# V cache loads issued from ScalarE's DMA queue, K cache loads from SyncE's

## Chip, cores, metric

One core of one Trainium2 chip runs the kernel; the other cores are idle. The metric is device time in microseconds (us) of one execution. Before: 1345.22 us (median of 4 runs, 1344.23 to 1347.4).

## The reference, cut

One decode step of grouped-query attention over a long cache, mixed with a small token MLP that takes almost no time here. Only the attention matters for the argument:

```python
# x [1,1,448], k_cache and v_cache [1, 8, 65536, 256] bfloat16, 16 query heads on 8 kv heads
q = (x @ wq)                                   # 16 heads x 256
p = softmax(einsum("bhqd,bhkd->bhqk", q, k) * 256**-0.5)
o = einsum("bhqk,bhkd->bhqd", p, v)
a = o.reshape(1, 1, 4096) @ wo
return g * a + (1 - g) * b                     # b: token MLP, g: a gate
```

K and V are 268 MB each. All of it must be read once, and nothing is reused.

## The kernel before

The cache is cut into 256 chunks of 2048 rows. Loads take two chunks at once (2 MB, 128 pieces of 16 KB, one for each partition). There are two K buffers (KB) and three V buffers (VB) of one load each. In step s, TensorE transposes the K of chunk s, multiplies q with the transposed K of chunk s-1 ("QK"), and multiplies the exponentials of chunk s-2 with V ("PV"):

```python
DC = 2; KB = 2; VB = 3; NB = 4                 # chunks per load; buffers; transpose groups per chunk
...
@block.sync                                    # SyncE issues every load
    ... six small loads, wq ...
    def k_dma(cd):                             # pair cd = chunks 2cd, 2cd+1
        if cd >= KB:
            eng.wait_ge(sem_tr, NB * ((cd - KB) * DC + DC))   # transposes of pair cd-2 done
        eng.dma_start(kbuf[slot cd % KB], ...).then_inc(sem_k[slot], 16)
    def v_dma(cd):
        if cd >= VB:
            eng.wait_ge(sem_pv, (cd - VB) * DC + DC)          # PV of pair cd-3 done
        eng.dma_start(vbuf[slot cd % VB], ...).then_inc(sem_v[slot], 16)
    for cd in range(NCD + 1):                  # K0, K1, V0, K2, V1, K3, V2, ...
        if cd < NCD: k_dma(cd)
        if cd - 1 >= 0: v_dma(cd - 1)
        ... at cd == NCD - 20: wo ...
@block.tensor
    for s in range(NC + 2):
        if s even: wait sem_k                  # K pair landed
        32 transposes of chunk s               # kst <- kbuf
        QK of chunk s-1                        # sps <- ktT
        if s even: wait sem_v                  # V pair landed
        PV of chunk s-2                        # po <- vbuf
@block.scalar                                  # half of the evictions of the transposes, and exp
    for c in range(NC):
        2 evictions of chunk c (ktT <- kst); exp of chunk c-1
```

So K(j+1) and V(j) are issued together, back to back, when the transposes of chunk 2j-1 are done.

The softmax here doesn't subtract the row's maximum and nothing guards it: scores larger than these inputs give would overflow.

Of the kernel before, what the change touches and what calls it, by code (L numbers as in the profile page):

```python
# [11 lines left out]
def bass_gated_mix__gqa_block_cached__mixer_token_mlp__decode_kernel(  # L12
# [29 lines left out]
    P = 128  # L42
    CH = 2048 if T % 2048 == 0 else T
# [3 lines left out]
    NCPH = T // CH  # L47
# [4 lines left out]
    DC = 2  # L52
    assert NC % DC == 0 and NCPH % DC == 0
    NCD = NC // DC
    KB = 2
    VB = 3
# [18 lines left out]
    with ctx:  # L75
        def sb(shape, dt, name):
            return ctx.enter_context(nc.sbuf_tensor(name, shape, dt))
# [4 lines left out]
        def new_sem(name):  # L82
            return ctx.enter_context(nc.semaphore(name))

        kbuf = sb([P, KB, DC, NT, DH], bf16, "kbuf")
        vbuf = sb([P, VB, DC, NT, DH], bf16, "vbuf")
# [52 lines left out]
        sem_v = [new_sem("semv%d" % i) for i in range(VB)]  # L139
# [9 lines left out]
        sem_pv = new_sem("sem_pv")  # L149
# [21 lines left out]
        @block.sync  # L171
        def _(eng):
            eng.dma_start(xrow_b[:, :], x_row_ap).then_inc(sem_misc, 16)
            eng.dma_start(grow_b[:, :], gate_w.rearrange("(a n) -> a n", a=1)).then_inc(sem_misc, 16)
            eng.dma_start(w1row_b[:, :], B_w1[0:1, :]).then_inc(sem_misc, 16)
            eng.dma_start(b1row_b[:, :], B_b1.rearrange("(a n) -> a n", a=1)).then_inc(sem_misc, 16)
            eng.dma_start(w2row_b[:, :], B_w2.rearrange("f a -> a f")).then_inc(sem_misc, 16)
            eng.dma_start(b2_b[:, :], B_b2.rearrange("(a n) -> a n", a=1)).then_inc(sem_misc, 16)
            eng.dma_start(wq_sb, A_wq.rearrange("(kt c) n -> c kt n", c=KCP)).then_inc(sem_wq, 16)

            def k_dma(cd):
                c0 = cd * DC
                g, k = divmod(c0, NCPH)
                slot = cd % KB
                if cd >= KB:
                    eng.wait_ge(sem_tr, NB * ((cd - KB) * DC + DC))
                src = A_k_cache[0, g, k * CH:(k + DC) * CH, :].rearrange("(p n) d -> p (n d)", p=P)
                eng.dma_start(kbuf[:, slot, :, :, :].rearrange("p c n d -> p (c n d)"), src).then_inc(sem_k[slot], 16)  # L188

            def v_dma(cd):  # L190
                c0 = cd * DC
                g, k = divmod(c0, NCPH)
                slot = cd % VB
                if cd >= VB:
                    eng.wait_ge(sem_pv, (cd - VB) * DC + DC)
                src = A_v_cache[0, g, k * CH:(k + DC) * CH, :].rearrange("(p n) d -> p (n d)", p=P)
                eng.dma_start(vbuf[:, slot, :, :, :].rearrange("p c n d -> p (c n d)"), src).then_inc(sem_v[slot], 16)  # L197

            WO_AT = max(0, NCD - 20)
            for cd in range(NCD + 1):  # L200
                if cd < NCD:
                    k_dma(cd)
                if cd - 1 >= 0:
                    v_dma(cd - 1)
                if cd == WO_AT:
                    eng.wait_ge(s_pe_pro, 3)
                    eng.dma_start(wo_sb, A_wo.rearrange("(kt p) n -> p kt n", p=P)).then_inc(sem_wo, 16)

            eng.wait_ge(sem_tail_v, 1)
            eng.dma_start(out_row_ap, out_b[:, :]).then_inc(sem_out, 16)  # L210
            eng.wait_ge(sem_out, 16)
# [261 lines left out]

        @block.scalar
        def _(act):
            act.wait_ge(s_d2a, 1)
            act.sqrt(statb[:, 3:4], statb[:, 2:3])
            act.activation(statb[:, 5:6], statb[:, 4:5], AF.Exp, scale=-1.0).then_inc(s_a2d, 1)

            def b_tanh(kt):  # L480
                slot = kt % NUR
                act.wait_ge(s_u, kt + 1)
                if kt >= NUR:
                    act.wait_ge(s_pb, kt - NUR + 1)
                act.activation(tring[:, slot, :], zring[:, slot, :], AF.Tanh  # L485
                               ).then_inc(s_tanh, 1)

            for c in range(NC):
                slotT = c % KTB
                if c >= KTB:  # L490
                    act.wait_ge(sem_qk, c - KTB + 1)
                for b in range(NB):
                    u2 = NB * c + b
                    if u2 % 2 != 1:
                        continue
                    act.wait_ge(sem_tr, u2 + 1)
                    act.activation(ktT[:, slotT, b, :], kst[:, b, :], AF.Copy).then_inc(sem_eva, 1)  # L497
                ce = c - 1
                if ce >= 0:
                    act.wait_ge(sem_qk, ce + 1)  # L500
                    if ce >= PTB:
                        act.wait_ge(sem_pv, ce - PTB + 1)
                    act.activation(pT[:, ce % PTB, :], sps[:, ce % 2, 0:2 * NT], AF.Exp, scale=scale  # L503
                                   ).then_inc(sem_exp, 1)
                if INTERLEAVE_B:
                    for kt in range(FT):
                        if posT[kt] == c:
                            b_tanh(kt)
            if not INTERLEAVE_B:
                for kt in range(FT):  # L510
                    b_tanh(kt)
            ce = NC - 1
            act.wait_ge(sem_qk, ce + 1)
            if ce >= PTB:
                act.wait_ge(sem_pv, ce - PTB + 1)
            act.activation(pT[:, ce % PTB, :], sps[:, ce % 2, 0:2 * NT], AF.Exp, scale=scale
                           ).then_inc(sem_exp, 1)
# [28 lines left out]
```

## Time and profile before

| what | where in the profile | value |
|---|---|---|
| time, median | timed runs | 1345.2 us |
| DMA share and rate, 60 to 1300 us | windows | 0.99 to 1.00, 407 to 418 GB/s |
| one 16 KB piece, median | the trace's DMA records | 611 ns |
| between landings of 2 MB loads, median | the trace's landings | 4.90 us |
| K and V, issue to landing, median | DMA issues | 10.6 and 15.2 us |

The page of the kernel before: span; busy time; the DMA queue (records, MB, share of 16 engines); the chain of work that ended last, by engine and by line; DMA issues (count, KB each, median us from issue to landing). PE is TensorE's matrix multiplications and PEld its weight loads, DVE is VectorE, ACT ScalarE, POOL GpSimd, SP SyncE; a q behind the name marks the engine's instruction queue, and "issue" is time in which the engine waited for nothing that the profile shows.

```profile
span 1353.2 us, 53303 instructions
...
PE 1190.9 (88%) x25055; PEld 1156.5 (85%) x25055; DVE 405.9 (30%) x690; ACT 549.1 (41%) x786; POOL 1.2 (0%) x10
...
q1 hardware_dynamic: 41454, 544.24, 97.3%
...
DMA 50%; PE 44%; issue 4%; SPq 1%; ACT 0%; DVE 0%; DVEq 0%; ACTq 0%
DMA vbuf<-in_A_v_cache_dram 50%; PE kst L277 28%; PE po L312 9%; PE sps L293 5%; PE den L316 1%; SPq L188 1%; PE sps L339 1%; PE po L322 0%; ACT ktT L497 0%; ACT pT L503 0%; SPq L197 0%; PE den L327 0%; DVE arow_b L467 0%; DVE densum L448 0%; DVE out_b L472 0%
...
kbuf<-in_A_k_cache_dram SPq DMA_DIRECT2D x128, 2048.0 KB, 10.6
vbuf<-in_A_v_cache_dram SPq DMA_DIRECT2D x128, 2048.0 KB, 15.2
wqo<-in_A_wq_dram SPq DMA_DIRECT2D x1, 3584.0 KB, 17.5
...
```

All loads go through one hardware queue (q1), which fills 97.3% of the 16 engines' time. V takes 4.6 us longer than K from issue to landing because it stands behind K in that queue.

Windows of the kernel before. After the stretch and its length come the busy time of each engine, the granted TensorE clock, the DMA share and GB/s:

```profile
...
core 0: us, PE busy (x) PEld busy (x) DVE busy (x) ACT busy (x) POOL busy (x), PEclk, DMA share, GB/s
60.00:200.00 140.00, 128.01 (x2697) 125.18 (x2695) 66.45 (x152) 62.74 (x93) 0.00 (x0) 0.73 1.00 418
200.00:600.00 400.00, 358.98 (x7665) 350.60 (x7664) 109.28 (x158) 166.58 (x237) 0.00 (x0) 0.75 1.00 417
600.00:1000.00 400.00, 361.28 (x7560) 350.64 (x7559) 107.12 (x156) 164.19 (x234) 0.00 (x0) 0.73 0.99 407
1000.00:1300.00 300.00, 261.01 (x5518) 255.38 (x5515) 78.87 (x114) 120.21 (x171) 0.00 (x0) 0.74 1.00 415
...
```

The engines have no time to spare. A load is 8 pieces per engine, and 8 x 611 ns is 4.89 us, just the median gap between landings. TensorE is busy 87 to 91% of the same windows, so it is close behind.

Who waited for whom (total us, times, longest us), and the chain of waits around 620 us (start us, us, what):

```profile
...
PE po L312 <- DMA vbuf<-in_A_v_cache_dram: 57.5, 56, 2.5
...
PE kst L277 <- DMA kbuf<-in_A_k_cache_dram: 12.1, 7, 9.6
...
```

```profile
...
618.27 0.33 SPq L188
618.60 0.04 issue
618.64 14.31 DMA vbuf<-in_A_v_cache_dram
632.95 0.14 issue
633.08 0.99 PE po L312 x32
...
```

TensorE hardly waits for K. It waits for V: the issue of K (0.33 us) and V, 14.31 us until V has landed, then PV.

The first transposes, from the timeline (start us, us, instruction, and in brackets the idle time before it and what ended it):

```profile
...
24.80 1.44 PE L277 MATMUL kst<-ident,kbuf 128*128 128x128 bf16 x12 [1.07 <-DMA kbuf<-in_A_k_cache_dram]
...
```

wq (3.5 MB) goes first, then K0; TensorE's main loop starts at 24.8 us.

### The profile page before, as it was taken

The numbers are of one execution on the slowest core, as the hardware profiler recorded it, in microseconds if no ns is written. First come the engines' busy times: TensorE is split into PE (matmuls) and PEld (weight loads), VectorE is DVE, ScalarE is ACT, GpSimd is POOL, SyncE is SP. The second block draws the span as 40 slices with busy tenths as digits, with TensorE's granted clock in tenths as the row PEclk, the third lists the DMA queues.
The fourth block names the chain that finished last, engine by engine and source line by source line (L and its number), as shares of the span: only waits on it lengthen the run. The fifth ranks groups of instructions, "written<-read, shape, count | busy, mean of one in ns | idle before, by whom it ended". The sixth has DMA issues, their size and how long they took to land.

```text
span 1353.2 us, 53303 instructions
## 1 busy us (share of the span) xinstructions
PE 1190.9 (88%) x25055; PEld 1156.5 (85%) x25055; DVE 405.9 (30%) x690; ACT 549.1 (41%) x786; POOL 1.2 (0%) x10
## 2 busy tenths in 40 slices
PE   4889898989989898989999888998899896888997
PEld 4889898889888898989888888888898896888886
DVE  3783222222222222222222222222222221222222
ACT  2454344434344344444434434433444442443442
POOL 0000000000000000000000000000000000000000
PEclk9677767768677778676787767766867767777777
DMA  9999999999999999999999999999999999999993
GB/s 302 425 423 411 417 419 425 409 422 412 420 416 416 420 405 423 418 420 407 414 399 402 409 404 414 416 382 402 420 422 419 409 423 398 421 417 416 414 417 160
DMA packets 41672, 547.65 MB, mean 405 GB/s; under 512 B 4136, under 2 KB 8235, under 8 KB 8238
## 3 DMA queue, kind: packets, MB, share of 16 engines
q1 hardware_dynamic: 41454, 544.24, 97.3%
q8 instruction: 198, 3.24, 0.9%
q14 instruction: 20, 0.16, 0.0%
HBM read 544.22 MB, written 0.00 MB: 402 GB/s over the span
## 4 chain that ended last, share of the span: by engine, by line
DMA 50%; PE 44%; issue 4%; SPq 1%; ACT 0%; DVE 0%; DVEq 0%; ACTq 0%
DMA vbuf<-in_A_v_cache_dram 50%; PE kst L277 28%; PE po L312 9%; PE sps L293 5%; PE den L316 1%; SPq L188 1%; PE sps L339 1%; PE po L322 0%; ACT ktT L497 0%; ACT pT L503 0%; SPq L197 0%; PE den L327 0%; DVE arow_b L467 0%; DVE densum L448 0%; DVE out_b L472 0%
## 5 line engine op out<-in xcount | busy, mean ns | idle before, releaser
L497 ACT ACTIVATE ktT<-kst 128x1024 bf16<-128x1024 bf16 x512 | 513.5, 1022 | 763.6 <-PE kst L277 763.6
L277 PE MATMUL kst<-ident,kbuf 128*128 128x128 bf16 x8192 | 726.0, 269 | 26.0 <-issue 13.7
L277 PEld LDWEIGHTS kst<-ident,kbuf 128*128 128x128 bf16 x8192 | 667.8, 125 | 38.5 <-issue 17.8
L433 DVE COPY ktT<-kst 128x1024 bf16<-128x1024 bf16 x512 | 352.9, 691 | 906.1 <-PE kst L277 894.8
L312 PE MATMUL po<-pT,vbuf 128*128 128x2 bf16 x8192 | 251.3, 164 | 92.2 <-DMA vbuf<-in_A_v_cache_dram 57.5
L312 PEld LDWEIGHTS po<-pT,vbuf 128*128 128x128 bf16 x8192 | 232.0, 99 | 98.3 <-issue 63.5
L293 PE MATMUL sps<-qT,ktT 128*128 128x2 bf16 x8192 | 255.6, 165 | 21.4 <-issue 21.2
L293 PEld LDWEIGHTS sps<-qT,ktT 128*128 128x128 bf16 x8192 | 250.6, 100 | 21.6 <-issue 21.4
L503 ACT ACTIVATE pT<-sps 128x32 bf16<-128x32 f32 x255 | 50.0, 196 | 16.0 <-PE sps L293 15.6
L316 PE MATMUL den<-pT,ones_col 128*1 128x32 bf16 x256 | 46.4, 181 | 0.0
L316 PEld LDWEIGHTS den<-pT,ones_col 128*1 128x1 bf16 x256 | 20.3, 79 | 7.5 <-issue 3.0
L254 PEld LDWEIGHTS sps<-xcol,wqo 112*128 112x128 bf16 x128 | 3.5, 104 | 8.2 <-issue 8.2
L254 PE MATMUL sps<-xcol,wqo 112*128 112x1 bf16 x128 | 3.6, 165 | 7.8 <-DMA wqo<-in_A_wq_dram 7.8
L339 PE MATMUL sps<-wqo,oTn 128*1 128x448 bf16 x32 | 8.1, 424 | 0.6 <-DVE oTn L460 0.6
L485 ACT ACTIVATE tring<-zring 128x448 bf16<-128x448 bf16 x14 | 8.1, 578 | 0.2 <-DVE zring L413 0.2
L339 PEld LDWEIGHTS sps<-wqo,oTn 128*1 128x1 bf16 x32 | 3.0, 98 | 5.3 <-issue 2.5
L244 PE MATMUL sps<-h_row,ones_row_b 1*128 1x448 bf16 x1 | 0.6, 551 | 6.5 <-DVE h_row L387 6.5
L405 DVE TENSOR_TENSOR wring<-uring 128x448 bf16<-128x448 bf16 x14 | 5.5, 393 | 1.4 <-issue 0.4
L407 DVE TENSOR_TENSOR zring<-wring,uring 128x448 bf16<-128x448 bf16 x14 | 5.5, 393 | 1.0
L422 DVE TENSOR_TENSOR gu<-wring,tring 128x448 bf16<-128x448 bf16 x14 | 5.5, 392 | 1.0
L411 DVE TENSOR_TENSOR zring<-uring,wring 128x448 bf16<-128x448 bf16 x14 | 5.5, 392 | 1.0
L244 PEld LDWEIGHTS sps<-h_row,ones_row_b 1*128 1x128 bf16 x1 | 0.1, 100 | 6.5 <-DVE h_row L387 6.5
(70 smaller groups left out, 51.0 us busy)
## 6 DMA issues: line engine op xcount, KB each, us to landing
kbuf<-in_A_k_cache_dram SPq DMA_DIRECT2D x128, 2048.0 KB, 10.6
vbuf<-in_A_v_cache_dram SPq DMA_DIRECT2D x128, 2048.0 KB, 15.2
wqo<-in_A_wq_dram SPq DMA_DIRECT2D x1, 3584.0 KB, 17.5
wqo<-in_A_wo_dram SPq DMA_DIRECT2D x1, 3584.0 KB, 24.9
xrow_b<-in_A_x_dram SPq DMA_DIRECT2D x1, 0.9 KB
grow_b<-in_gate_w_dram SPq DMA_DIRECT2D x1, 0.9 KB
w1row_b<-in_B_w_dram SPq DMA_DIRECT2D x1, 3.5 KB
b1row_b<-in_B_b_dram SPq DMA_DIRECT2D x1, 3.5 KB
```

The source lines that it names most:

```text
L188: eng.dma_start(kbuf[:, slot, :, :, :].rearrange("p c n d -> p (c n d)"), src).then_inc(sem_k[slot], 16)
L254: ins = pe.matmul(sps[:, 1, j:j + 1], wq_sb[0:KCP, kt, col0:col0 + P], xcol[0:KCP, kt:kt + 1], start=(kt == 0), stop=(kt == KC - 1))
L277: ins = pe.transpose(kst[:, b, j * P:(j + 1) * P], kbuf[:, slot, ck, nt, dh * P:(dh + 1) * P], ident[:, :])
L293: ins = pe.matmul(sps[:, sbk, 2 * nt:2 * nt + 2], ktT[:, slotT, bnk, j * P:(j + 1) * P], qT[:, dh, REP * g:REP * g + REP], start=(dh == 0) ...
L312: pe.matmul(po[:, col:col + REP], vbuf[:, vslot, cv, nt, dh * P:(dh + 1) * P], pT[:, pslot, 2 * nt:2 * nt + 2], start=first, stop=last)
L316: ins = pe.matmul(den[0:1, g * 2 * NT:(g + 1) * 2 * NT], ones_col[:, 0:1], pT[:, pslot, 0:2 * NT], start=(k == 0), stop=(k == NCPH - 1))
L339: ins = pe.matmul(sps[0:1, 1, 0:DM], oTn[:, col:col + 1], wo_sb[:, kt, :], start=(i == 1), stop=(i == nmm))
L405: vec.tensor_tensor(W, U, U, op=ALU.mult)
L433: vec.tensor_copy(ktT[:, slotT, b, :], kst[:, b, :]).then_inc(sem_evd, 1)
L485: act.activation(tring[:, slot, :], zring[:, slot, :], AF.Tanh).then_inc(s_tanh, 1)
L497: act.activation(ktT[:, slotT, b, :], kst[:, b, :], AF.Copy).then_inc(sem_eva, 1)
L503: act.activation(pT[:, ce % PTB, :], sps[:, ce % 2, 0:2 * NT], AF.Exp, scale=scale).then_inc(sem_exp, 1)
```

## The change

The intent: two rings (a ring is here the work that one issuing engine has queued for the 16 DMA engines; the profile lists each as a hardware queue, q1 or q10) feed the 16 engines at once. V moves to ScalarE's queue. To fit ScalarE's program, V(j) is issued after ScalarE's evictions of chunk 2j-2, one step earlier than before; the first three V loads are issued at the very start.

```diff
@@ SyncE @@
-            def v_dma(cd): ...                # as above
-            for cd in range(NCD + 1):
-                if cd < NCD:
-                    k_dma(cd)
-                if cd - 1 >= 0:
-                    v_dma(cd - 1)
+            for cd in range(NCD):
+                k_dma(cd)
                 if cd == WO_AT: ...
@@ ScalarE @@
+            def v_dma(cd): ...                # the same, with act.wait_ge and act.dma_start
+            for cd in range(min(VB, NCD)):
+                v_dma(cd)
             act.wait_ge(s_d2a, 1)
...
                     act.activation(ktT[:, slotT, b, :], kst[:, b, :], AF.Copy).then_inc(sem_eva, 1)
+                if c % DC == 0 and VB <= c // DC + 1 < NCD:
+                    v_dma(c // DC + 1)
```

More of the change, by code (lines that the diff above doesn't have):

```diff
@@ L188, in k_dma @@
                 eng.dma_start(kbuf[:, slot, :, :, :].rearrange("p c n d -> p (c n d)"), src).then_inc(sem_k[slot], 16)
-            def v_dma(cd):
-                c0 = cd * DC
-                g, k = divmod(c0, NCPH)
-                slot = cd % VB
-                if cd >= VB:
-                    eng.wait_ge(sem_pv, (cd - VB) * DC + DC)
-                src = A_v_cache[0, g, k * CH:(k + DC) * CH, :].rearrange("(p n) d -> p (n d)", p=P)
-                eng.dma_start(vbuf[:, slot, :, :, :].rearrange("p c n d -> p (c n d)"), src).then_inc(sem_v[slot], 16)
-            WO_AT = max(0, NCD - 20)
-            for cd in range(NCD + 1):
-                if cd < NCD:
-                    k_dma(cd)
-                if cd - 1 >= 0:
-                    v_dma(cd - 1)
+            WO_AT = max(0, NCD - 20)
+            for cd in range(NCD):
+                k_dma(cd)
                 if cd == WO_AT:
@@ L475, in _, with v_dma @@
         def _(act):
+            def v_dma(cd):
+                c0 = cd * DC
+                g, k = divmod(c0, NCPH)
+                slot = cd % VB
+                if cd >= VB:
+                    act.wait_ge(sem_pv, (cd - VB) * DC + DC)
+                src = A_v_cache[0, g, k * CH:(k + DC) * CH, :].rearrange("(p n) d -> p (n d)", p=P)
+                act.dma_start(vbuf[:, slot, :, :, :].rearrange("p c n d -> p (c n d)"), src).then_inc(sem_v[slot], 16)
+            for cd in range(min(VB, NCD)):
+                v_dma(cd)
             act.wait_ge(s_d2a, 1)
```

## The prediction

> **What bounds the kernel now.** The loads. Windows over 60 to 1300 us give a DMA share of 0.99 to 1.00 at 407 to 418 GB/s. In the packed trace the 16 KB packets of the cache loads take 611 ns (median), so 8 per engine make a 2 MB load 4.89 us; the median gap between successive landings of cache loads is 4.90 us, the mean 5.14. So the rings run without bubbles; lost are slow packets (about 41 us per engine in all), the two 3.5 MB weight loads, and the ends. TensorE is busy 1191 us (88%) at a mean granted clock of 0.74, near 9.2 us of the 10.3 us that a K/V pair takes; it pauses about 1 us per pair at the P·V matmul (L312, timeline), and the chain of waits alternates V load (50%) and TensorE (44%). SyncE is no limit: 0.33 us (K) and 0.43 us (V) per issue, and it waited 1190 us at L188.
>
> **What the change does.** 128 V issues move from SyncE to ScalarE: 125 in the loop, about 0.43 us each, 54 us on an engine busy 549 us, ahead of an exp with over 2 us of slack. Nearly nothing of it is critical. Bytes and buffers stay. [...]
>
> What moves:
> 1. V(j) is issued about one step (5 us) earlier relative to TensorE, after the transposes of chunk 2j-2 instead of 2j-1. With two rings taking turns, K and V each get about half the rate while both are outstanding: a load then takes about 2 x 4.9 = 9.8 us. V landing falls from 15.2 to 10-12 us, K stays near 10 (10.6 now). TensorE's wait moves from V (57 us listed, more under exp and issue) to K (12 us now).
> 2. Start: three V loads (6 MB) compete with wq and K0. K0 landed at 24.7 us; I estimate 31 to 37. V buffers are then full and loads idle a few us: about +4, less about 2 for the earlier first load.
> 3. End: before, the last load was V, landing at 1335.3, TensorE's loop ending 4.3 us later. Now K(127) lands about when V(127) does, and two chunks of transposes follow: about +5.
> 4. Slow packets cluster 1 to 3 us after an issue. Two rings may fill such holes (up to -35 us if all went) or conflict more. I take -6.
>
> Sum: 1346 + 2 + 5 - 6 = about 1347 us. 80% range 1320 to 1370. Chances: faster by over 2% 0.12, within 2% 0.77, slower by over 2% 0.11.
>
> **What would show it.** Right: DMA share still 0.99-1.00 and 405-425 GB/s in the steady windows; two busy hardware queues of equal bytes; 16 KB packets recorded at about 1.2 us; TensorE's waits for V under 20 us and for K at L277 above 60; first transposes after 30 us; V landing 10-12 us. Wrong: windows where the DMA share falls under 0.95 in mid-kernel, or a steady rate above 425 or under 395 GB/s.
>
> **What would make it wrong.** Two read streams at once disturbing HBM or the engines (slower); the second ring hiding the slow packets (faster); unfair turns that starve K until V's buffers are full and the engines idle; ScalarE held at an issue.

The turns of two rings (item 1) and the 1.2 us for a piece were assumptions. The trace of the change, taken later, shows what there is of them: while both rings held 16 KB pieces not yet started (853 of the 1000 us from 100 to 1100 us), K's ring started 12.8 and V's 11.9 per us; the median piece took 611 ns.

## The result

The change took 1401.58 us (median of 4, 1389.84 to 1405.52) against 1345.22 us. The ratio is 1.0406 (95% interval 1.0361 to 1.0452): slower by 4%. The result lies outside the predicted range of 1320 to 1370 us.

The page after (lines of the program have moved by 12: L277 is L265, L312 is L300):

```profile
span 1397.9 us, 53303 instructions
...
PE 1150.2 (82%) x25055; PEld 1119.1 (80%) x25055; DVE 405.9 (29%) x690; ACT 546.2 (39%) x786; POOL 1.2 (0%) x10
...
q1 hardware_dynamic: 23022, 275.80, 48.0%
q10 hardware_dynamic: 18432, 268.44, 47.9%
...
DMA 56%; PE 43%; issue 1%; DVE 0%; SPq 0%; DVEq 0%
DMA kbuf<-in_A_k_cache_dram 56%; PE kst L265 30%; PE po L300 5%; PE sps L281 5%; PE den L304 1%; PE sps L327 1%; PE po L310 0%; PE den L315 0%; DVE arow_b L455 0%; DVE densum L436 0%; DVE out_b L460 0%; SPq L179 0%; SPq L173 0%; DVE t1row L457 0%; SPq L178 0%
...
vbuf<-in_A_v_cache_dram ACTq DMA_DIRECT2D x128, 2048.0 KB, 12.9
kbuf<-in_A_k_cache_dram SPq DMA_DIRECT2D x128, 2048.0 KB, 12.4
wqo<-in_A_wq_dram SPq DMA_DIRECT2D x1, 3584.0 KB, 35.8
...
```

Two queues (q1 and q10) share the engines half and half. K now needs 12.4 us to land, where 10.6 was measured before and about 10 predicted. The chain that ended last runs through K loads (56%) instead of V loads (50%), as one would expect when TensorE's wait moves to K. wq lands after 35.8 us instead of 17.5.

Windows after, in the columns of those before:

```profile
...
60.00:200.00 140.00, 121.39 (x2659) 118.92 (x2657) 75.76 (x182) 63.98 (x96) 0.00 (x0) 0.76 0.98 402
200.00:600.00 400.00, 339.73 (x7338) 332.70 (x7336) 103.86 (x151) 158.10 (x227) 0.00 (x0) 0.74 0.98 401
600.00:1000.00 400.00, 342.25 (x7486) 333.55 (x7485) 106.51 (x155) 161.36 (x231) 0.00 (x0) 0.78 0.99 407
1000.00:1300.00 300.00, 246.55 (x5409) 241.43 (x5408) 77.34 (x112) 117.33 (x168) 0.00 (x0) 0.78 0.99 400
...
```

The rate fell from 407 to 418 down to 400 to 407 GB/s, and the DMA share to 0.98 and 0.99. Averaged with their lengths as weights, these windows moved 413.4 GB/s before and 402.8 GB/s after, 2.6% less; over 1240 us that is about 32 us. About half of this is idle engines (the unrounded DMA share fell from 1.000 to 0.987), the other half slower pieces (on average 629 ns before and 638 ns after in these windows). On the whole TensorE was granted no lower a clock than before (0.74 to 0.78 against 0.73 to 0.75), so its pace is not the cause. (The table of landings below gives 20 us in the middle and 9 around wo in place of these 32.)

```profile
...
PE kst L265 <- DMA kbuf<-in_A_k_cache_dram: 131.2, 67, 16.4
...
PE po L300 <- issue: 40.1, 35, 2.3
...
```

```profile
...
602.25 10.75 DMA kbuf<-in_A_k_cache_dram
612.99 0.04 issue
613.04 3.59 PE kst L265 x32
...
618.43 3.54 PE kst L265 x32
621.97 0.02 issue
621.99 11.94 DMA kbuf<-in_A_k_cache_dram
...
```

The wait moved from V to K, and more than doubled. The chain is now a loop: K is issued, lands 10.75 us later, two chunks are transposed in 9 us, which frees the buffer, and the next K is issued.

```profile
...
43.23 3.04 PE L265 MATMUL kst<-ident,kbuf 128*128 128x128 bf16 x27 [1.13 <-DMA kbuf<-in_A_k_cache_dram]
...
```

TensorE's loop starts 18.4 us later than before. Where the time went can be counted in landed loads, of K and V together, in the two traces:

| nth landing of a 2 MB load | before, us | after, us | lag, us |
|---|---|---|---|
| 17th | 105.5 | 120.9 | 15 |
| 211th | 1096.9 | 1131.6 | 35 |
| 226th (wo came in between) | 1182.5 | 1226.6 | 44 |
| 256th, the last | 1335.3 | 1376.6 | 41 |
| end | 1353.2 | 1397.9 | 45 |

About 15 us are lost at the start, 20 in the middle, 9 around wo, and 4 after the last landing; 3 were won back between the 226th landing and the last. The profiled execution of before (span 1353.2 us; a span is some 1.8 us shorter than the timed execution) was some 10 us longer than the median of its timed runs, and that of the change 2 us shorter, which is why these lags sum to 45 and not to the 56 us between the medians. E1 below, one ring and as fast as the kernel before, has a profile near its median (1342.3 us). Against its landings the change lags 15 us at the 17th, 48 at the 211th, 57 at the 226th and 57 at the end: then some 33 us are lost in the middle, not 20.

### The profile page after: what moved, and what is told of

The parts are those of the page before. It is cut to its first block, busy times and chain, and to the rows that moved or that the text cites. A ratio compares the mean times of both kernels' runs of the same rounds, so it can differ in the third digit from the quotient of the medians.

```text
span 1397.9 us, 53303 instructions
## 1 busy us (share of the span) xinstructions
PE 1150.2 (82%) x25055; PEld 1119.1 (80%) x25055; DVE 405.9 (29%) x690; ACT 546.2 (39%) x786; POOL 1.2 (0%) x10
## 4 chain that ended last, share of the span: by engine, by line
DMA 56%; PE 43%; issue 1%; DVE 0%; SPq 0%; DVEq 0%
DMA kbuf<-in_A_k_cache_dram 56%; PE kst L265 30%; PE po L300 5%; PE sps L281 5%; PE den L304 1%; PE sps L327 1%; PE po L310 0%; PE den L315 0%; DVE arow_b L455 0%; DVE densum L436 0%; DVE out_b L460 0%; SPq L179 0%; SPq L173 0%; DVE t1row L457 0%; SPq L178 0%
## 5 line engine op out<-in xcount | busy, mean ns | idle before, releaser
L265 PE MATMUL kst<-ident,kbuf 128*128 128x128 bf16 x8192 | 697.4, 263 | 142.9 <-DMA kbuf<-in_A_k_cache_dram 131.2
L265 PEld LDWEIGHTS kst<-ident,kbuf 128*128 128x128 bf16 x8192 | 643.2, 121 | 157.4 <-DMA kbuf<-in_A_k_cache_dram 136.6
L300 PE MATMUL po<-pT,vbuf 128*128 128x2 bf16 x8192 | 248.6, 163 | 40.3 <-issue 40.1
L281 PE MATMUL sps<-qT,ktT 128*128 128x2 bf16 x8192 | 252.2, 164 | 23.4 <-issue 22.8
L281 PEld LDWEIGHTS sps<-qT,ktT 128*128 128x128 bf16 x8192 | 245.9, 99 | 23.3 <-issue 22.4
L300 PEld LDWEIGHTS po<-pT,vbuf 128*128 128x128 bf16 x8192 | 228.8, 97 | 42.0 <-issue 41.8
L242 PE MATMUL sps<-xcol,wqo 112*128 112x1 bf16 x128 | 3.6, 165 | 17.9 <-DMA wqo<-in_A_wq_dram 17.9
L242 PEld LDWEIGHTS sps<-xcol,wqo 112*128 112x128 bf16 x128 | 3.5, 104 | 18.4 <-issue 18.4
L221 PE MATMUL den<-one_b,xrow_b 1*112 1x1 bf16 x4 | 0.5, 232 | 11.9 <-DMA b_b<-in_B_b_dram 11.9
L221 PEld LDWEIGHTS den<-one_b,xrow_b 1*112 1x112 bf16 x4 | 0.4, 197 | 11.9 <-DMA b_b<-in_B_b_dram 11.9
## 6 DMA issues: line engine op xcount, KB each, us to landing
vbuf<-in_A_v_cache_dram ACTq DMA_DIRECT2D x128, 2048.0 KB, 12.9
kbuf<-in_A_k_cache_dram SPq DMA_DIRECT2D x128, 2048.0 KB, 12.4
wqo<-in_A_wq_dram SPq DMA_DIRECT2D x1, 3584.0 KB, 35.8
```

The costliest lines, as they stand in the source:

```text
L242: ins = pe.matmul(sps[:, 1, j:j + 1], wq_sb[0:KCP, kt, col0:col0 + P], xcol[0:KCP, kt:kt + 1], start=(kt == 0), stop=(kt == KC - 1))
L265: ins = pe.transpose(kst[:, b, j * P:(j + 1) * P], kbuf[:, slot, ck, nt, dh * P:(dh + 1) * P], ident[:, :])
L281: ins = pe.matmul(sps[:, sbk, 2 * nt:2 * nt + 2], ktT[:, slotT, bnk, j * P:(j + 1) * P], qT[:, dh, REP * g:REP * g + REP], start=(dh == 0) ...
L300: pe.matmul(po[:, col:col + REP], vbuf[:, vslot, cv, nt, dh * P:(dh + 1) * P], pT[:, pslot, 2 * nt:2 * nt + 2], start=first, stop=last)
```

## The experiments

Theory A: **the two rings share the engines, so a V load issued later overtakes part of an earlier K load. K lands later, and with two K buffers the loop from K's landing to the next K issue becomes the limit.** The overtaking can be counted in the trace of the change: for each K load issued from 100 to 1100 us, 9 to 117 pieces (median 40) of V loads issued after it started before its own last piece did. Rivals: B, the separate, earlier place of the V issue does it, with any number of rings; B', two rings make the engines slower in themselves; C, the late start is the whole of it. The experiments ran on four chips, each with the kernel before in its own rounds; its medians there were 1342.5 to 1346.8 us, so that differences of medians between rounds are uncertain by a few us.

### E1, E2, E3, E4

E1 keeps one ring and takes over only the place:

```diff
-            for cd in range(NCD + 1):
-                if cd < NCD: k_dma(cd)
-                if cd - 1 >= 0: v_dma(cd - 1)
+            k_dma(0); k_dma(1); v_dma(0)
+            for cd in range(1, NCD):
+                eng.wait_ge(sem_tr, NB * ((cd - 1) * DC + 1))   # transposes of chunk 2cd-2
+                v_dma(cd)
+                if cd + 1 < NCD: k_dma(cd + 1)
```

> All loads on SyncE's ring as before, but V(j) is issued where the change issues it (after the transposes of chunk 2j-2, one step before K(j+1)). Theory A (K shares the engines packet by packet with V, lands later, and with two K buffers K's loop of issue, landing and transposes becomes the limit): the single ring keeps loads in turn, so 1340 to 1356 us. Theory B (it is the separate place of the issues: a V load now goes ahead of K[...]): 1365 to 1400 us, with slow-packet time near 56 us per engine instead of 36.

Measured: 1342.53 us, ratio 0.997 (0.991 to 1.003). Its windows from 200 to 1000 us:

```profile
...
200.00:600.00 400.00, 354.55 (x7734) 346.87 (x7731) 109.44 (x160) 166.88 (x239) 0.00 (x0) 0.77 1.00 419
600.00:1000.00 400.00, 355.35 (x7757) 346.52 (x7756) 110.67 (x160) 167.49 (x240) 0.00 (x0) 0.78 1.00 418
...
```

The place costs nothing on one ring, so rival B falls: the slow pieces took 26 us per engine, where B expected 56 (an assumption). K's landing took 12.7 us here too (median, from the trace), and TensorE waited 117 us for K; yet the engines stayed full:

```profile
...
PE kst L280 <- DMA kbuf<-in_A_k_cache_dram: 116.8, 93, 11.8
...
```

Even the chain that ended last is the one of the change: K loads 56%, TensorE 43%. So neither the later landing of K nor this chain tells the loss by itself. The late K did no harm in E1, where no issue between 100 and 1100 us found less than 1.1 us of issued work left (the count is explained at E6).

E2 undoes only the start of the change:

```diff
-            for cd in range(min(VB, NCD)): v_dma(cd)            # at the top of ScalarE's program
...
+            act.wait_ge(sem_k[0], 16)                           # after the prelude: K0 has landed
+            for cd in range(min(VB, NCD)): v_dma(cd)
```

> The change, but ScalarE issues its first three V loads only after K0 has landed, so that wq and K0 have the engines alone. By the count of loads landed, the change is about 15 us behind at the 16th load. If that start is lost for good: about 1385 us (15 us less than the change), first transposes at about 25 us. If the loop in mid-kernel sets the time and the start only shifts it, the same. If the start were the whole cause: 1346 us.

Measured: 1393.82 us, ratio 1.0353 (1.0293 to 1.0414). K0 landed at 24.3 us. The 14 us won by the 17th landing (106.8 us, against 120.9 for the change) had shrunk to 8 by the last, and the expected 1385 us was missed by 9. Rival C falls: the start is a small part.

E3 gives the change a third K buffer, E4 gives the kernel before one:

```diff
-    KB = 2
+    KB = 3
```

> The change with three K buffers in place of two. Theory A (K's loop over two buffers): the loop gets a pair more of room, TensorE's waits for K in mid-kernel vanish and the rate from 200 to 1000 us returns to 413 GB/s or more; time about 1360 us, what is left being the start. Theory B' (two rings make the engines themselves slower): rate stays at 400 to 407 GB/s, time above 1385 us.

> Control for the third K buffer: the kernel before with three K buffers. Its engines are already busy 99 to 100% of the middle, so a deeper buffer should give little under every theory: 1330 to 1346 us.

Measured: E3 1351.81 us, ratio 1.0035 (0.9985 to 1.0084); E4 1338.47 us, ratio 0.9938 (0.9889 to 0.9987). E3's windows and its wait for K:

```profile
...
200.00:600.00 400.00, 358.33 (x7703) 350.95 (x7701) 110.42 (x160) 168.64 (x239) 0.00 (x0) 0.76 1.00 419
600.00:1000.00 400.00, 362.32 (x7645) 352.02 (x7645) 108.41 (x157) 165.54 (x235) 0.00 (x0) 0.74 1.00 417
...
```

```profile
...
PE kst L265 <- DMA kbuf<-in_A_k_cache_dram: 13.4, 2, 12.3
...
```

A third K buffer wins back 50 of the 56 us (E3 was expected at about 1360). With it, two rings move as much as one: 419 and 417 GB/s, in E1 419 and 418. Rival B' falls. The waits for K shrank from 131 to 13 us.

### E5 to E8

E5 is E3 with E2's gated start.

> Two rings, three K buffers, and the first V loads gated behind K0. If the change's loss is the sum of the K loop (about 50 us, won back by the third K buffer) and the late start (about 7 to 13 us), both undone give 1336 to 1346 us, level with the one-ring kernel with three K buffers (1338). If something of the second ring itself remains: 1350 us or more.

Measured: 1346.86 us, ratio 1.0027 (1.0012 to 1.0042), which is just above the range expected for "both undone" and 8 us above E4 (12 us by the ratios). Its last load landed at 1322.6 us, E4's at 1321.1; the ends are 1345.3 and 1337.0. So about 7 of the 8 us lie behind the last landing, in TensorE's work that was still to be done; loading was level with one ring.

E6 issues V(j) on ScalarE's queue, with the gated start, at the place of the kernel before:

```diff
-                if c % DC == 0 and VB <= c // DC + 1 < NCD:
+                if c % DC == DC - 1 and c // DC + 1 < NCD:
                     v_dma(c // DC + 1)
```

(At the start only V0 is issued, after K0 has landed.)

> Two rings with gated start, but V(j) is issued where the kernel before issues it, after the transposes of chunk 2j-1, at the same moment as K(j+1). This is the fourth corner of ring by place; early V on one ring was 1342. Theory A (turn-taking between the rings with too little K buffer): the place doesn't matter, 1380 to 1405 us. Rival (only the early place together with a second ring hurts): 1345 to 1360 us.

Measured: 1463.50 us, ratio 1.0891 (1.0856 to 1.0927). The direction is theory A's, but the statement "the place doesn't matter" is wrong: 70 us more than E2. This is the clearest picture of the mechanism. Its windows, and its chain of waits:

```profile
...
200.00:600.00 400.00, 323.43 (x7071) 316.69 (x7070) 100.29 (x146) 151.80 (x219) 0.00 (x0) 0.77 0.95 382
600.00:1000.00 400.00, 324.70 (x7042) 316.37 (x7041) 100.56 (x146) 151.88 (x218) 0.00 (x0) 0.77 0.96 384
...
```

```profile
...
607.04 13.77 DMA kbuf<-in_A_k_cache_dram
620.80 0.05 issue
620.85 3.26 PE kst L265 x32
...
625.80 1.91 PE kst L265 x32
627.71 0.02 issue
627.72 14.88 DMA kbuf<-in_A_k_cache_dram
...
```

K is issued at 627.72 us and lands 14.88 us later. The trace's list of issues and landings says why:

```text
kernel before                  the change                     E6
K 690.14 -> 701.81             V 605.84 -> 618.75             K 616.93 -> 631.36
V 690.51 -> 706.70             K 609.59 -> 621.81             V 616.94 -> 631.53
K 700.95 -> 711.59             V 616.68 -> 626.69             K 627.72 -> 642.60
V 701.32 -> 716.93             K 621.99 -> 633.93             V 627.74 -> 642.76
```

On one ring K lands about 5 us ahead of the V issued with it (median 4.90 us in the trace of before). In E6 the two land 0.17 us apart (median): K has waited for V's bytes. While both rings held work they moved 12.1 and 11.7 pieces per us (in the change 12.8 and 11.9), so each got about half, and in short turns: of the loads issued at 640 us neither was ever more than 13 pieces ahead, less than one for each engine. From a landing of K to the next issue into its buffer TensorE needs some 7 to 9 us (median 7.2 in E6, 8.7 in the change). On one ring the V behind that K (4.9 us) and the whole next pair (9.8 us) can be moved meanwhile; in E6 only the next pair. In the trace of the change 47 loads were issued to an empty ring (the one before had landed): the earliest first piece started 0.97 us after the start of the issue, 0.64 us after its end; the median from the start was 1.1 us for V and 1.5 for K. So 9.8 us of issued work must cover some 8 to 10 us, and the rings run dry: at 45% of E6's K issues between 100 and 1100 us, less than 1.1 us of issued work was left (pieces issued and not started, times 611 ns, over 16 engines). Before, it was 4% of the K issues; in the change none of the K issues and 15% of the V issues; in E1 and E3 none at all. At 641.0 us in E6, for example, only 6 of the 16 engines were moving pieces, 0.6 us after an issue.

This also says what the early place does in the change: K and V are issued half a period apart, so that one helps to cover the gap of the other. It made the change better than E6, not worse.

E7 spends the 16 KB per partition of the third K buffer on a fourth V buffer instead:

```diff
-    VB = 3
+    VB = 4
...
-                if c % DC == 0 and VB <= c // DC + 1 < NCD:
-                    v_dma(c // DC + 1)
+                if c % DC == 0 and VB <= c // DC + 2 < NCD:
+                    v_dma(c // DC + 2)
```

> The change with a fourth V buffer (the same 16 KB per partition that the third K buffer cost), V issued one pair earlier, K left at two buffers. If what counts is K's own loop (two buffers, landing in 12.4 us under competition): no gain, 1390 us or more, with waits for K of 130 us or more. If what counts is only that the engines run out of issued packets (mean backlog 1.14 loads against 1.54 before): the deeper V ring keeps them busy, 1350 to 1370 us.

Measured: 1402.28 us, ratio 1.0437 (1.0389 to 1.0485), no gain over the change.

```profile
...
PE kst L265 <- DMA kbuf<-in_A_k_cache_dram: 145.3, 66, 14.7
...
```

Between 200 and 1000 us it moved 406 and 403 GB/s, about as the change (401 and 407). So it is K's loop that counts, not the bytes of buffer in all.

E8 halves the loads (1 MB, four K and six V buffers, the same bytes):

```diff
-    DC = 2; KB = 2; VB = 3
+    DC = 1; KB = 4; VB = 6
...
+                if VB <= c + 3 < NCD:
+                    v_dma(c + 3)
```

> The change with loads of 1 MB (one chunk) instead of 2 MB, in four K and six V buffers, so the same buffer bytes and the same order, but each K buffer is freed and refilled after one chunk. Theory A: a load in competition takes half as long and a buffer is given back twice as often, so the loop is no limit: 1345 to 1365 us, what remains being the start. If two rings were slow in themselves: 1390 us or more.

Measured: 1363.27 us, ratio 1.0148 (1.0127 to 1.0169). Of the 56 us, 38 come back with the same buffer bytes. Halved loads have a price of their own, which E10 measures.

### E9 to E12

E9 uses both rings for every load, in the order of the kernel before. Chunk 0 of each load goes to SyncE's queue, chunk 1 to ScalarE's:

```diff
+ SyncE:    dma_start(kbuf[:, slot, 0], src[:, 0:16, :]);  dma_start(vbuf[:, slot, 0], ...)
+ ScalarE:  dma_start(kbuf[:, slot, 1], src[:, 16:32, :]); dma_start(vbuf[:, slot, 1], ...)   # same waits, same order
```

(ScalarE's first ones wait for wq. TensorE waits for 32 instead of 16 per load.) E10 issues the same halves from SyncE alone. (Cut from E9's expectation is an inference about order that no trace shows by itself; TensorE's waits in E9 are listed as 58 us for V and 30 for K.)

> Both rings hold work all the time, but each load is cut in half, one half on each ring, issued in the order and at the places of the kernel before (two K and three V buffers). [...] If the order of the loads is the cause: 1340 to 1356 us. If two rings in use at once with two K buffers hurt in whatever order: 1385 us or more.

> Control for the halves: the kernel before with each load issued as two halves (8 KB runs instead of 16 KB) on SyncE alone. 1342 to 1352 us under every theory; what it costs over the kernel before is the price of the smaller loads and twice the issues.

Measured: E9 1368.72 us, ratio 1.0162 (1.0125 to 1.0199); E10 1357.34 us, ratio 1.0082 (1.0050 to 1.0113). Both missed their ranges: halves cost more than was allowed for. An 8 KB piece took 318 ns on average in both, so two of them took 637 ns, where one 16 KB piece of the cache took 629 on average in the kernel before. Against its control, the second ring costs E9 11 us. From 200 to 1000 us the rates are 413 and 412 GB/s (E9) and 414 and 413 (E10), with a DMA share of 1.01 in each, so these 11 us are not lost there. K0's second half, which had to wait for wq, landed at 29.95 us, in E10 at 24.73. Counted in landings E9 is 4.8 us behind at the 8th half load, 4.4 at the 256th (674 us in E10), 5.0 at the 384th (1001 us), and 9.5 at the last. The windows from 600 to 1000 us, E9 and then E10:

```profile
...
600.00:1000.00 400.00, 357.89 (x7595) 347.58 (x7594) 107.83 (x156) 167.30 (x236) 0.00 (x0) 0.77 1.01 412
...
600.00:1000.00 400.00, 360.76 (x7645) 350.50 (x7643) 108.61 (x157) 165.88 (x237) 0.00 (x0) 0.73 1.01 413
...
```

So with the order of issue kept, two rings in use at once and two K buffers did no harm in the middle. The last 5 us are lost around wo: E9 is 5.2 us behind at the 432nd half load (1128 us in E9) and 9.2 at the 450th (1189 us). E9 keeps more than the order, though: between 200 and 1000 us each issue found pieces in its own ring that had not started (11 at the least), where 46% of the change's issues found none. So E9 does not tell the lost order apart from the start gap of an empty ring.

E11 is E4 again, for a closer interval.

> The fastest version so far, again with more rounds: one ring, three K buffers. Ratio to the kernel before 0.990 to 0.998.

Measured: 1340.09 us, ratio 0.9951 (0.9926 to 0.9976). It is the fastest version here: half a per cent ahead of the kernel before, clear of noise, below the 2% that would be called faster.

E12 is E6 with a third K buffer.

> The slowest version (two rings, V issued late, together with K: 1463 us) with a third K buffer. If its loss is K's loop (K lands together with V, so that the transposes overlap with only one pair of loads, and the rings run dry), a further pair issued ahead keeps the rings filled: 1342 to 1360 us, and the share of issues that find under 1.1 us of work left falls from 46% to under 5%. If two loads issued in parallel are slow for another reason: above 1400 us.

Measured: 1365.71 us, ratio 1.0165 (1.0139 to 1.0191). One K buffer wins 98 us. It ended 6 us above the expected range, and 9% of the K issues still found under 1.1 us of work left (45% in E6 by this count; the 46% quoted there was counted over K loads 12 to 101).

| run | rings | K buffers | V place | median us | ratio |
|---|---|---|---|---|---|
| before | 1 | 2 | late | 1345.22 | 1 |
| E1 | 1 | 2 | early | 1342.53 | 0.997 |
| the change | 2 | 2 | early | 1401.58 | 1.041 |
| E2 (gated start) | 2 | 2 | early | 1393.82 | 1.035 |
| E6 (gated start) | 2 | 2 | late | 1463.50 | 1.089 |
| E7 (4 V buffers) | 2 | 2 | one pair earlier | 1402.28 | 1.044 |
| E3 | 2 | 3 | early | 1351.81 | 1.004 |
| E5 (gated start) | 2 | 3 | early | 1346.86 | 1.003 |
| E12 (gated start) | 2 | 3 | late | 1365.71 | 1.017 |
| E4, E11 | 1 | 3 | late | 1338.47, 1340.09 | 0.994, 0.995 |
| E8 (1 MB loads) | 2 | 4 halves | early | 1363.27 | 1.015 |
| E9, halves on both rings | 2 | 2 | late | 1368.72 | 1.016 |
| E10, halves on one ring | 1 | 2 | late | 1357.34 | 1.008 |

## Why the prediction was wrong

Held: the loads bound the kernel, and no bandwidth was to be had by a second ring (E3 on two rings 419 and 417 GB/s, E1 on one 419 and 418). ScalarE's issues were harmless: one takes 0.33 us, and ScalarE was busy 546 us after and 549 before. TensorE's wait moved from V to K (none listed for V, 131 us for K). Two queues carried the same bytes. The end was mis-sized only slightly: from the last landing to the end it took 21.3 us after and 17.9 before, 3.4 us more where 5 were predicted.

Wrong:

1. **The step that failed is the first of "What moves": "With two rings taking turns, K and V each get about half the rate while both are outstanding ... K stays near 10", joined to "DMA share still 0.99-1.00".** That the rings would share the engines was foreseen, but not what this does to order. The prediction took rings that never run empty as given, although that held for the order on one ring. K landed after 12.4 us, V after 12.9 (10 to 12 predicted); the share fell to 0.98 and 0.99 and the rate by 2.6%, about 32 us, for which the sum had no term; slow packets stood in it as a gain ("I take -6"). The late landing alone is no loss: in E1 K landed after 12.7 us, on a ring that stayed full. A third K buffer (E3) wins back 50 us and the full rate, a fourth V buffer (E7) nothing, the same place on one ring (E1) loses nothing, and two rings in the old order (E9 against E10) lose nothing in the middle. So the loss comes from two rings sharing the engines (12.8 and 11.9 pieces per us) between loads that are needed at different times, together with too few K buffers: at the next issue too little work is left. None of the prediction's own signs of being wrong (a share under 0.95, a rate under 395 GB/s) showed in these windows; 2.6% over 1240 us was enough.
2. **The start was mis-sized.** The prediction had first transposes at 31 to 37 us and a net cost of 2 us (+4 and -2). They came at 43.2 us, and 15 us of loading were lost by the 17th landing. Undone alone (E2) it is worth 8 us in the medians; undone beside a third K buffer (E5 against E3), 5 us, or nothing that can be told from noise by the ratios (1.0027 and 1.0035, each to the kernel before in its own rounds).
3. **The recorded pieces.** The expected 1.2 us for a 16 KB piece did not show: the median stayed 611 ns. Nor were there two pieces for each engine under way at once: of the cache's and weights' pieces in the change, between 60 and 1300 us, never more than 22 were recorded in progress on the 16 engines, most often 16 (69% of the time). Slow pieces (the sum of what each took over 611 ns, per engine) rose from 35 to 50 us between 60 and 1300 us, where a gain of 6 had been assumed. In E1 and E3, whose rings never ran dry, they stay near 26 and 28. In E6, where the rings ran driest, they took 65 us. That slow pieces follow from rings that have run dry fits, but was not tested alone; it is about half of the 32 us.

The cause is settled as far as these runs go: a second ring against the depth of K's buffers. That the order of delivery does it, and not in part the start gap of a ring that has run empty, is argued from E6's landings and not tested alone. Left open are why E2's 14 us shrank to 8, how much of the 9 us around wo has a cause of its own (K(109)'s issue on SyncE took 18 us behind wo's 4096 small pieces; before, 11.5 us; with a third K buffer, E3, nearly nothing is lost there: 86.9 us from the 211th to the 226th landing, against 85.7 before and 95.0 in the change; but E9 loses some 4 us there with the order kept), and pauses of 1 to 2 us inside TensorE's groups that the profile lists as "issue".

## What to carry to other kernels

In these runs the DMA engines were full (share 0.99 to 1.00 before), and a second queue added no bandwidth (400 to 407 GB/s in the change, 417 and 419 in E3, 407 to 418 before); it only replaced "in the order of issue" by "in turns", so that the load needed first landed later, together with the other (E6: K after 14.7 us, V after 14.8; on one ring 10.6 and 15.2). Before splitting streams over queues, ask which load is needed first and whether there are enough buffers for all of them to land at the end; if the kernel lives on two buffers, as here, keep the loads on one ring in the order of need. A wait that moves from one load to another is not yet a loss (E1): look at whether work is left in the rings when the next issue comes.
